# The last stage's weights made float32 a stage earlier, and operands at equal addresses

## The chip, the cores and the metric

The kernel runs on one core of a Trainium2 chip. The metric is the device time of one execution in microseconds (us); several executions are timed and their median counts.

## The reference

Eight batches of eight heads, 576 tokens of 64 values each. Keys and values are averaged over groups of 8 tokens, so each head has 72 keys. All inputs are float32 except the weights' storage: they arrive as float64 words.

```python
k_p = k.reshape(B, H, Sp, 8, D).mean(axis=3); v_p = v.reshape(B, H, Sp, 8, D).mean(axis=3)
attn = softmax(scale * q @ k_p.T)
x = (attn @ v_p)            # (4608 tokens, 512)
h = max(x @ w1, x @ w2, x @ w3)     # 512 -> 768
x = h @ w_out                       # 768 -> 512
h = x @ w_in2                       # 512 -> 2048
out = (h - tanh(h)) @ w_out2        # 2048 -> 512
```

## The kernel before

Every product is taken in three matmuls on float32r parts: an operand is split into a high part H (a cast on ScalarE) and a low part L (value minus H, on VectorE or GpSimd), and the products H·H, H·L and L·H are accumulated. A weight tile arrives as 128 x 512 float64 words (512 KB); `conv` makes it float32 with one VectorE pass for the exponent (L78), a ScalarE pass on it (L80), four VectorE passes for sign and mantissa (L81, L83, L85, L87), then the cast to H (L89) and the subtraction for L (L90, on GpSimd).

The work is in three stages, one after the other on TensorE.

- **Stage A** computes attention and the maximum of the three products, in 12 blocks of 384 tokens. `moe_group` (L476 to L482) is one group of 12 matmuls of 384 columns; a block has 18 groups. The attention's steps stand in one list, written out by hand, and `moe_part` spreads them between the groups (`pace`), about two blocks ahead; they are over before block 10 begins. A tile of 128 tokens takes four score products (`qk`, L240 and L242, added up on VectorE at L245), a softmax (L263 to L272), transposes (`tr_main` at L288, `tr_left`) and, per unit of tiles, four products with the values (`av`). The first 18 groups convert the 18 weight tiles of the three products, the last block converts the 6 tiles of `wo1`. The results h go to DRAM (`hs`).
- **Stage B** (from the heading "phase B" in the code) is the product h @ w_out in 9 blocks of 512 tokens. A block has 6 groups, one per input chunk of 128; a group is 12 matmuls of 512 columns into four PSUM banks (L592 to L594). The h tile of a group is loaded four groups ahead and split two groups ahead (`load_split`, L561, L566, L567). Between the groups `conv_c` converts the 32 weight tiles of stage C, `win` and `wout` in turn, into the 32 pairs `wt`, where they stay. The results x go to DRAM (`xs`) from four copies each block (L598 on ScalarE, L600 on VectorE).
- **Stage C** takes 9 blocks of 512 tokens, 16 chunks of 128 inner columns each. `h2` (L662 to L664) is 12 matmuls of the weights' `ct` tiles (stationary) with the x tiles `ioH` and `ioL` (moving), into one bank. `gact` makes g = h - tanh(h) on ScalarE and VectorE. `prod` (L675 to L677), three chunks later, is 12 matmuls of g (stationary) with the `ct` tiles (moving) into four banks. The x tiles of a block are split on GpSimd.

The tile framework orders the instructions of each engine from the order of the code and the readiness that its planner expects; each engine then runs its own list in order. All loads and stores are issued by one queue, SyncE's.

SBUF is filled from two sides. The left side begins behind 16,384 bytes of scratch and some constants and holds, in A, the weights of the three products, the x tiles and the conversion's tiles; in C the `ct` tiles, from byte 16,576 of each partition. The right side grows down from byte 229,344: in A all of attention, in B and C first the pool `io` (ioL, ioH, ob), then `wo` (B) or `gp` (the g tiles, C). All tiles of `io`, `wo`, `wl` and `gp` have sizes that are multiples of 512 bytes.

Of the kernel before, what the change touches and what calls it, by code (L numbers as in the profile page):

```python
# [47 lines left out]
def moe_chain_kernel(ctx, tc, qt, kt, vm, vl, ident, cst, w123, wo1, win, wout, out):  # L48
# [18 lines left out]

    # float64 words to float32, split into two float32r parts
    def conv_load(st, src):
# [3 lines left out]

    def conv(st, raw, H, L, eng):
        pe = st.tile([128, 512], I32, tag="pe", name="pe", bufs=2)
        a = st.tile([128, 512], I32, tag="ma", name="ma", bufs=2)
        lo, hi = raw[:, :, 0], raw[:, :, 1]
        V.tensor_scalar(out=pe, in0=hi, scalar1=20, scalar2=0x7FF,  # L78
                        op0=ALU.logical_shift_right, op1=ALU.bitwise_and)
        A.activation(pe, pe, AF.Relu, bias=ebias, scale=float(1 << 23))  # L80
        V.tensor_scalar(out=a, in0=hi, scalar1=3, scalar2=0x7FFFFF,  # L81
                        op0=ALU.logical_shift_left, op1=ALU.bitwise_and)
        V.scalar_tensor_tensor(out=a, in0=hi, scalar=-2147483648, in1=a,  # L83
                               op0=ALU.bitwise_and, op1=ALU.bitwise_or)
        V.scalar_tensor_tensor(out=a, in0=lo, scalar=29, in1=a,  # L85
                               op0=ALU.logical_shift_right, op1=ALU.bitwise_or)
        V.tensor_tensor(out=a, in0=a, in1=pe, op=ALU.bitwise_or)  # L87
        w = a.bitcast(F32)
        A.copy(H, w)  # L89
        eng.tensor_tensor(out=L, in0=w, in1=H.bitcast(F32), op=ALU.subtract)  # L90

# [1 line left out]
    cp = pool("cst")  # L93
    wa = pool("wa")
    xr = pool("xr", bufs=3)
    hp = pool("hp", bufs=4)
    sta = pool("sta")
    at = pool("at", side="right")

# [16 lines left out]

    # attention units: (first token, tiles of tokens); a tile is (batch, first token in batch, count)
    units = []
# [199 lines left out]

    # one list of steps for the whole attention, in the order in which they are issued
    steps = []  # L320
# [84 lines left out]
    for o in tail:  # L405
        add(*o)
    # v of a batch may be replaced once its last product is issued
    done_at = {}
# [15 lines left out]

    # startup
    for t in (kbd[0], VX, VH, VL, kbd[1]):
# [18 lines left out]
    def conv_next():  # L445
        i = nconv[0]
        if i < 18:
            conv(sta, raws.pop(i), wH[i].rearrange("p a b -> p (a b)"),
                 wL[i].rearrange("p a b -> p (a b)"), G)
            nconv[0] += 1  # L450
            if i + 2 < 18:
                raws[i + 2] = conv_load(sta, w123[i + 2])

    first_av = next(i for i, (f, _) in enumerate(steps) if f is av)
# [33 lines left out]

    def moe_part(groups, upto):
        """groups of products, with the attention's steps up to upto spread over them"""  # L490
        first = pos[0]

        def pace(x):
            attn_to(first + (upto - first) * x // (2 * len(groups)))

        for k, (j, f, m) in enumerate(groups):
            conv_next()
            moe_group(j, f, m, lambda: pace(2 * k + 1))
            pace(2 * k + 2)
# [6 lines left out]
    def point(x):  # L506
        """the step at which the attention is x blocks far"""
        j = int(x)
        if j >= NA - 1:
            return len(steps) - 1  # L510
        lo = block_end[j - 1] if j else -1
        return int(lo + (block_end[j] - lo) * (x - j)) if x > j else lo
# [4 lines left out]
    for j in range(2, NA - 1):  # L517
        moe_part(gr(j), point(j + 2 + LEAD))
    attn_to(len(steps) - 1)
    close("at")  # L520
    io = pool("io", side="right")
# [15 lines left out]
    for nme in ("sta", "hp", "xr", "wa"):  # L537
        close(nme)

# [1 line left out]
    wl = pool("wl")  # L541
    stb = pool("stb", side="right")
    wt = [(wl.tile([128, 512], F32R, name=f"ctH{c}"), wl.tile([128, 512], F32R, name=f"ctL{c}"))
          for c in range(2 * NC2)]
    # pairs in the order of use: input chunk c, output chunk c
    srcs = [(win if c % 2 == 0 else wout)[c // 2] for c in range(2 * NC2)]
    raws = {i: conv_load(stb, srcs[i]) for i in range(2)}
    nconv = [0]

    def conv_c():  # L550
        i = nconv[0]
        if i < 2 * NC2:
            conv(stb, raws.pop(i), wt[i][0], wt[i][1], G)
            nconv[0] += 1
            if i + 2 < 2 * NC2:
                raws[i + 2] = conv_load(stb, srcs[i + 2])

# [14 lines left out]
    def hsrc(j, kc):  # L572
        g, o = divmod(j * BB, HG)
        return hs[g][kc][:, o:o + BB]

    loads = [(j, kc) for j in range(NB) for kc in range(NF)]
    AHEAD, SPL = 4, 2
# [5 lines left out]
    for i, (j, kc) in enumerate(loads):  # L583
        if kc == 0:
            acc = [psm.tile([128, 512], F32, tag="mm", name="ps_mm") if j % 2 == 0 else
                   ps2.tile([128, 512], F32, tag="sc" if e < 2 else "tr", name="ps_acc") for e in range(NE)]
# [15 lines left out]
        if i + AHEAD < len(loads):  # L602
            lt[i + AHEAD] = load_split(hsrc(*loads[i + AHEAD]), V)
        while nconv[0] < min(2 * NC2, (i + 1) * 2 * NC2 // (len(loads) - 2)):
            conv_c()
    close("stb")
    close("wo")
# [3 lines left out]

# [1 line left out]
    gp = pool("gp", bufs=2, side="right")  # L613
    xl_ = [(j, kc) for j in range(NB) for kc in range(NE)]
    lt = {}
    nld, nsp = [0], [0]

    def c_load():
        i = nld[0]
        if i < len(xl_):  # L620
            j, kc = xl_[i]
            lt[i] = load_split(xs[j][kc], G)
            nld[0] += 1

    def c_split():
        i = nsp[0]
        if i < len(xl_):
            lt[i][1]()
            nsp[0] += 1

    def gact(ps):
# [25 lines left out]
    def h2(j, c):  # L657
        ps = psc.tile([128, 512], F32, tag="mm", name="ps_mm", bufs=3)
        wh, wl_ = (t.rearrange("p (a b) -> p a b", b=128) for t in wt[2 * c])
        for kc in range(NE):  # L660
            xh, xl2 = lt[j * NE + kc][0]
            T.matmul(ps, wh[:, kc], xh, start=(kc == 0), stop=False)  # L662
            T.matmul(ps, wh[:, kc], xl2, start=False, stop=False)  # L663
            T.matmul(ps, wl_[:, kc], xh, start=False, stop=(kc == NE - 1))  # L664
        return ps
# [20 lines left out]

    for _ in range(4):
        c_load()
    for _ in range(4):
        c_split()  # L690
    seq = [(j, c) for j in range(NB) for c in range(NC2)]
    for i in range(len(seq) + LAG):
# [5 lines left out]
        if i < len(seq):  # L698
            gs[j, c] = gact(ps)
            if c == 2:  # L700
                for _ in range(NE):
                    c_load()
            if 6 <= c < 10:
                c_split()
            if c == NC2 - 1:
                for k in range(NE):
                    lt.pop(j * NE + k)
    for nme in ("psc", "gp", "io", "wl", "cst"):
        close(nme)
# [54 lines left out]
```

## Time and profile before

| | |
|---|---|
| Median of 3 runs | 1609.07 us (1609.0 to 1609.45) |
| Profiled execution, first to last instruction | 1608.5 us |
| Busy: TensorE / VectorE / ScalarE / GpSimd | 1548.1 / 1215.2 / 836.4 / 223.7 us |
| Mean granted TensorE clock | 0.990 |
| Moved by DMA | 117.87 MB |

The span of the profile is the time on the core between the first and the last instruction; around it lie 0.6 us up to the median of the timed runs. Matmuls are pipelined, so that TensorE's busy time counts overlaps of neighbours; the distance from one start to the next tells more. "Granted clock" is the share of full speed (2.4 GHz) that the throttle lets through; its other level is 0.5.

### The profile page before, as it was taken

To read this page: it belongs to the slowest core of one execution; us is meant where nothing else is said; L and a number is where in the kernel's file an instruction comes from. 1 tells how busy PE (TensorE), PEld (TensorE's weight loads), DVE (VectorE), ACT (ScalarE), POOL (GpSimd) and SP (SyncE) were. 2 spreads that over 40 slices of the span, in tenths; PEclk is the share of its full clock that TensorE was granted. 3 is DMA by queue.
4 is the path that set the end of the run, shared out by engine and by line. 5 is a ranking of instruction groups with operands and counts; after the bars stand their busy time and mean duration, and the time that the engine had idled before them with its cause. 6 is when DMAs were issued, how large, how long until landed. Compare 5 with 4: busy or idle time off the path is not lost.

```text
span 1608.5 us, 21497 instructions
## 1 busy us (share of the span) xinstructions
PE 1548.1 (96%) x7540; PEld 1337.7 (83%) x7540; DVE 1215.2 (76%) x2131; ACT 836.4 (52%) x2081; POOL 223.7 (14%) x245
## 2 busy tenths in 40 slices
PE   4789999999999999998899999999999999999999
PEld 4688999999999999876688888888888888888887
DVE  8999565555555663999588878788888888887886
ACT  5565455545545521444465555555555555555554
POOL 5351210202010011332301001010101001010000
PEclk9899999999999999999999999999999999999999
DMA  7455232212121232676500001010100000010000
GB/s 236 158 161 163 84 99 79 87 45 75 42 65 39 67 120 77 230 241 234 198 1 27 26 2 52 1 53 0 33 21 27 26 27 27 1 54 0 27 1 27
DMA packets 61997, 117.87 MB, mean 73 GB/s; under 512 B 10816, under 2 KB 20160, under 8 KB 61888
## 3 DMA queue, kind: packets, MB, share of 16 engines
q1 hardware_dynamic: 61888, 116.49, 21.8%
q8 instruction: 59, 0.97, 0.3%
q14 instruction: 50, 0.41, 0.1%
HBM read 83.43 MB, written 33.03 MB: 72 GB/s over the span
## 4 chain that ended last, share of the span: by engine, by line
PE 50%; DVE 0%; issue 0%
PE ps_mm L663 8%; PE ps_mm L662 8%; PE ps_mm L664 8%; PE ps_acc L676 8%; PE ps_acc L675 8%; PE ps_acc L677 8%; DVE ob L683 0%
## 5 line engine op out<-in xcount | busy, mean ns | idle before, releaser
L476 PE MATMUL ps_mm<-xH,wH 128*128 128x384 f32 x864 | 304.5, 353 | 5.3 <-ACT wH L89 4.5
L477 PE MATMUL ps_mm<-xL,wH 128*128 128x384 f32 x864 | 292.4, 339 | 1.0 <-DVE xL L317 1.0
L478 PE MATMUL ps_mm<-xH,wL 128*128 128x384 f32 x864 | 292.7, 339 | 0.6 <-POOL wL L90 0.6
L650 ACT CAST gH<-w 128x512 fp32r<-128x512 f32 x144 | 89.4, 621 | 297.0 <-DVE w L649 297.0
L662 PE MATMUL ps_mm<-ioH,ctH 128*128 128x512 f32 x576 | 228.3, 396 | 5.3 <-ACT ob L598 5.3
L663 PE MATMUL ps_mm<-ioL,ctH 128*128 128x512 f32 x576 | 229.1, 398 | 0.0
L664 PE MATMUL ps_mm<-ioH,ctL 128*128 128x512 f32 x576 | 228.5, 397 | 0.0
L675 PE MATMUL ps_acc<-ctH,gH 128*128 128x512 f32 x576 | 228.1, 396 | 0.0
L676 PE MATMUL ps_acc<-ctL,gH 128*128 128x512 f32 x576 | 227.9, 396 | 0.0
L677 PE MATMUL ps_acc<-ctH,gL 128*128 128x512 f32 x576 | 227.9, 396 | 0.0
L651 DVE TENSOR_TENSOR gL<-w,gH 128x512 fp32r<-128x512 f32 x144 | 104.1, 723 | 92.5 <-ACT gH L650 92.3
L476 PEld LDWEIGHTS ps_mm<-xH,wH 128*128 128x128 f32 x864 | 164.7, 191 | 7.2 <-ACT wH L89 4.8
L477 PEld LDWEIGHTS ps_mm<-xL,wH 128*128 128x128 f32 x864 | 164.6, 191 | 1.9 <-DVE xL L317 1.7
L478 PEld LDWEIGHTS ps_mm<-xH,wL 128*128 128x128 f32 x864 | 163.7, 189 | 1.5 <-POOL wL L90 1.5
L567 POOL TENSOR_TENSOR ioL<-ioL,ioH 128x512 fp32r<-128x512 f32 x36 | 53.5, 1509 | 666.9 <-ACT ioH L566 666.9
L662 PEld LDWEIGHTS ps_mm<-ioH,ctH 128*128 128x128 f32 x576 | 108.6, 189 | 32.2 <-ACT ob L598 5.7
L663 PEld LDWEIGHTS ps_mm<-ioL,ctH 128*128 128x128 f32 x576 | 108.7, 189 | 27.1
L664 PEld LDWEIGHTS ps_mm<-ioH,ctL 128*128 128x128 f32 x576 | 108.8, 189 | 26.0
L675 PEld LDWEIGHTS ps_acc<-ctH,gH 128*128 128x128 f32 x576 | 108.2, 188 | 26.5
L677 PEld LDWEIGHTS ps_acc<-ctH,gL 128*128 128x128 f32 x576 | 108.2, 188 | 26.5
L676 PEld LDWEIGHTS ps_acc<-ctL,gH 128*128 128x128 f32 x576 | 108.2, 188 | 25.8
L482 DVE TENSOR_TENSOR h<-h,ps_mm 128x384 f32<-128x384 f32 x144 | 79.0, 549 | 66.0 <-PE ps_mm L478 59.2
(108 smaller groups left out, 2924.9 us busy)
## 6 DMA issues: line engine op xcount, KB each, us to landing
hs<-h SPq DMA_DIRECT2D x72, 192.0 KB, 1.9
ioL<-hs SPq DMA_DIRECT2D x54, 256.0 KB, 4.2
kraw<-kt SPq DMA_DIRECT2D x32, 288.0 KB, 3.9
raw<-w SPq DMA_DIRECT2D x18, 512.0 KB, 3.5
xs<-ob SPq DMA_DIRECT2D x36, 256.0 KB, 2.6
ioL<-xs SPq DMA_DIRECT2D x36, 256.0 KB, 3.0
out<-ob SPq DMA_DIRECT2D x36, 256.0 KB, 2.2
qraw<-qt SPq DMA_DIRECT2D x32, 256.0 KB, 2.7
```

The costliest lines, as they stand in the source:

```text
L476: T.matmul(ps[:, :BA], wH[i][:, kc], xh[:, kc], start=(kc == 0), stop=False)
L477: T.matmul(ps[:, :BA], wH[i][:, kc], xl[:, kc], start=False, stop=False)
L478: T.matmul(ps[:, :BA], wL[i][:, kc], xh[:, kc], start=False, stop=(kc == NE - 1))
L482: V.tensor_tensor(out=t, in0=t, in1=ps[:, :BA], op=ALU.max)
L650: A.copy(gH, w)
L651: V.tensor_tensor(out=gL, in0=w, in1=gH.bitcast(F32), op=ALU.subtract)
L662: T.matmul(ps, wh[:, kc], xh, start=(kc == 0), stop=False)
L663: T.matmul(ps, wh[:, kc], xl2, start=False, stop=False)
L664: T.matmul(ps, wl_[:, kc], xh, start=False, stop=(kc == NE - 1))
L675: T.matmul(acc, gH[:, r], oh, start=(c == 0), stop=False)
L676: T.matmul(acc, gH[:, r], ol, start=False, stop=False)
L677: T.matmul(acc, gL[:, r], oh, start=False, stop=(c == NC2 - 1))
```

## The change

`conv` is cut in two: `conv_bits` makes the float32 word on VectorE and ScalarE, and the split into H and L is apart. In stage A a new `conv_store` loads the raw words of stage C's weights, makes them float32 and stores them to DRAM (`wsc`, 256 KB a tile); it is called before every fourth group of blocks 2 to 10. In stage B `w_load` brings one such tile a group into the place of its L part, and `w_split` casts it (ScalarE) and subtracts (GpSimd).

The loads and splits of stage C's first x tiles move into the last groups of B, where nothing of h is left to load, and these four are subtracted on VectorE. The accumulators of B's blocks swap their two sets of PSUM banks, so that the last block uses the other four.

The scratch at the start of SBUF goes from 16,384 to 1,024 bytes, and a pad of 72 float32 words is put at the outer end of the right side.

```diff
@@ -65,13 +65,17 @@
     hs = [dr.tile([NF, 128, HG], F32, name=f"hs{i}") for i in range(NT // HG)]
     xs = [dr.tile([NE, 128, BB], F32, name=f"xs{i}") for i in range(NB)]

+    srcs = [(win if c % 2 == 0 else wout)[c // 2] for c in range(2 * NC2)]
+    wsc = [dr.tile([128, 512], F32, name=f"wsc{i}") for i in range(2 * NC2)]
     def conv_load(st, src):
         raw = st.tile([128, 512, 2], I32, tag="raw", name="raw", bufs=2)
         Q.dma_start(out=raw.bitcast(I64).rearrange("p n o -> p (n o)"), in_=src)
         return raw

-    def conv(st, raw, H, L, eng):
+    def conv_bits(st, raw):
         pe = st.tile([128, 512], I32, tag="pe", name="pe", bufs=2)
         a = st.tile([128, 512], I32, tag="ma", name="ma", bufs=2)
         lo, hi = raw[:, :, 0], raw[:, :, 1]
...
@@ -85,16 +89,21 @@
         V.scalar_tensor_tensor(out=a, in0=lo, scalar=29, in1=a,
                                op0=ALU.logical_shift_right, op1=ALU.bitwise_or)
         V.tensor_tensor(out=a, in0=a, in1=pe, op=ALU.bitwise_or)
-        w = a.bitcast(F32)
+        return a
+    def conv(st, raw, H, L, eng):
+        w = conv_bits(st, raw).bitcast(F32)
         A.copy(H, w)
         eng.tensor_tensor(out=L, in0=w, in1=H.bitcast(F32), op=ALU.subtract)

     cp = pool("cst")
     wa = pool("wa")
     xr = pool("xr", bufs=3)
     hp = pool("hp", bufs=4)
     sta = pool("sta")
+    pool("rp", side="right").tile([128, 72], F32, name="rpad")
     at = pool("at", side="right")

     consts = cp.tile([128, 12], F32, name="consts")
...
@@ -450,6 +459,19 @@
             nconv[0] += 1
             if i + 2 < 18:
                 raws[i + 2] = conv_load(sta, w123[i + 2])
+    nws = [0, 0]
+    craw = {}
+    def conv_store():
+        i = nws[0]
+        if i < 2 * NC2:
+            craw[i] = conv_load(sta, srcs[i])
+            nws[0] += 1
+        i = nws[1]
+        if i in craw and (i + 1 in craw or nws[0] == 2 * NC2):
+            Q.dma_start(out=wsc[i], in_=conv_bits(sta, craw.pop(i)).bitcast(F32))
+            nws[1] += 1

     first_av = next(i for i, (f, _) in enumerate(steps) if f is av)
     attn_to(NP)
...
@@ -495,6 +517,8 @@

         for k, (j, f, m) in enumerate(groups):
             conv_next()
+            if store and k % store == store - 1:
+                conv_store()
             moe_group(j, f, m, lambda: pace(2 * k + 1))
             pace(2 * k + 2)

...
@@ -515,8 +539,10 @@
     moe_part(gr(1, 0, HF), point(2.5))
     moe_part(gr(0, HF, NF) + gr(1, HF, NF), point(3 + LEAD))
     for j in range(2, NA - 1):
-        moe_part(gr(j), point(j + 2 + LEAD))
+        moe_part(gr(j), point(j + 2 + LEAD), 4)
     attn_to(len(steps) - 1)
+    while nws[1] < 2 * NC2:
+        conv_store()
     close("at")
     io = pool("io", side="right")
     wo = pool("wo", side="right")
...
@@ -537,23 +563,24 @@
     for nme in ("sta", "hp", "xr", "wa"):
         close(nme)

     wl = pool("wl")
-    stb = pool("stb", side="right")
     wt = [(wl.tile([128, 512], F32R, name=f"ctH{c}"), wl.tile([128, 512], F32R, name=f"ctL{c}"))
           for c in range(2 * NC2)]
-    srcs = [(win if c % 2 == 0 else wout)[c // 2] for c in range(2 * NC2)]
-    raws = {i: conv_load(stb, srcs[i]) for i in range(2)}
-    nconv = [0]
-    def conv_c():
-        i = nconv[0]
+    nw = [0, 0]
+    def w_load():
+        i = nw[0]
         if i < 2 * NC2:
-            conv(stb, raws.pop(i), wt[i][0], wt[i][1], G)
-            nconv[0] += 1
-            if i + 2 < 2 * NC2:
-                raws[i + 2] = conv_load(stb, srcs[i + 2])
+            Q.dma_start(out=wt[i][1].bitcast(F32), in_=wsc[i])
+            nw[0] += 1
+    def w_split():
+        i = nw[1]
+        h, l = wt[i]
+        A.copy(h, l.bitcast(F32))
+        G.tensor_tensor(out=l, in0=l.bitcast(F32), in1=h.bitcast(F32), op=ALU.subtract)
+        nw[1] += 1

     def load_split(src, eng):
         l = io.tile([128, 512], F32R, tag="L", name="ioL", bufs=8)
...
@@ -572,6 +599,23 @@
     def hsrc(j, kc):
         g, o = divmod(j * BB, HG)
         return hs[g][kc][:, o:o + BB]
+    xl_ = [(j, kc) for j in range(NB) for kc in range(NE)]
+    ct = {}
+    nld, nsp = [0], [0]
+    def c_load(eng):
+        i = nld[0]
+        if i < len(xl_):
+            j, kc = xl_[i]
+            ct[i] = load_split(xs[j][kc], eng)
+            nld[0] += 1
+    def c_split():
+        i = nsp[0]
+        if i < len(xl_):
+            ct[i][1]()
+            nsp[0] += 1

     loads = [(j, kc) for j in range(NB) for kc in range(NF)]
     AHEAD, SPL = 4, 2
...
@@ -582,7 +626,7 @@
         lt[i][1]()
     for i, (j, kc) in enumerate(loads):
         if kc == 0:
-            acc = [psm.tile([128, 512], F32, tag="mm", name="ps_mm") if j % 2 == 0 else
+            acc = [psm.tile([128, 512], F32, tag="mm", name="ps_mm") if j % 2 else
                    ps2.tile([128, 512], F32, tag="sc" if e < 2 else "tr", name="ps_acc") for e in range(NE)]
         (h, l), _ = lt.pop(i)
         if i + SPL < len(loads):
...
@@ -601,33 +645,21 @@
                 Q.dma_start(out=xs[j][e], in_=ob)
         if i + AHEAD < len(loads):
             lt[i + AHEAD] = load_split(hsrc(*loads[i + AHEAD]), V)
-        while nconv[0] < min(2 * NC2, (i + 1) * 2 * NC2 // (len(loads) - 2)):
-            conv_c()
-    close("stb")
+        else:
+            c_load(V)
+        if i >= len(loads) - 2:
+            c_split()
+            c_split()
+        w_load()
+        while nw[1] < min(2 * NC2, i * 2 * NC2 // (len(loads) - 4)):
+            w_split()
     close("wo")
     close("ps2")
     close("psm")
     psc = pool("psc", space=PS)

     gp = pool("gp", bufs=2, side="right")
-    xl_ = [(j, kc) for j in range(NB) for kc in range(NE)]
-    lt = {}
-    nld, nsp = [0], [0]
-    def c_load():
-        i = nld[0]
-        if i < len(xl_):
-            j, kc = xl_[i]
-            lt[i] = load_split(xs[j][kc], G)
-            nld[0] += 1
-    def c_split():
-        i = nsp[0]
-        if i < len(xl_):
-            lt[i][1]()
-            nsp[0] += 1
     def gact(ps):
         u = gp.tile([128, 512], F32, tag="u", name="u")
         th = gp.tile([128, 512], F32, tag="th", name="th")
...
@@ -658,7 +690,7 @@
         ps = psc.tile([128, 512], F32, tag="mm", name="ps_mm", bufs=3)
         wh, wl_ = (t.rearrange("p (a b) -> p a b", b=128) for t in wt[2 * c])
         for kc in range(NE):
-            xh, xl2 = lt[j * NE + kc][0]
+            xh, xl2 = ct[j * NE + kc][0]
             T.matmul(ps, wh[:, kc], xh, start=(kc == 0), stop=False)
             T.matmul(ps, wh[:, kc], xl2, start=False, stop=False)
             T.matmul(ps, wl_[:, kc], xh, start=False, stop=(kc == NE - 1))
...
@@ -684,10 +716,6 @@
                 r0 = j * BB + t * 128
                 Q.dma_start(out=out[r0:r0 + 128, :], in_=ob)

-    for _ in range(4):
-        c_load()
-    for _ in range(4):
-        c_split()
     seq = [(j, c) for j in range(NB) for c in range(NC2)]
     for i in range(len(seq) + LAG):
         if i < len(seq):
...
@@ -699,13 +727,13 @@
             gs[j, c] = gact(ps)
             if c == 2:
                 for _ in range(NE):
-                    c_load()
+                    c_load(G)
             if 6 <= c < 10:
                 c_split()
             if c == NC2 - 1:
                 for k in range(NE):
-                    lt.pop(j * NE + k)
-    for nme in ("psc", "gp", "io", "wl", "cst"):
+                    ct.pop(j * NE + k)
+    for nme in ("psc", "gp", "io", "rp", "wl", "cst"):
         close(nme)


...
@@ -753,7 +781,7 @@
         "w123": c(w123), "wo1": c(moe_w_out).view(np.int64).reshape(NF, 128, 512),
         "win": cols(moe2_w_in), "wout": c(moe2_w_out).view(np.int64).reshape(NC2, 128, 512),
     }
-    nc = bacc.Bacc("TRN2", target_bir_lowering=False, num_devices=1)
+    nc = bacc.Bacc("TRN2", target_bir_lowering=False, num_devices=1, dynamic_dma_scratch_size=1024)
     args = [nc.dram_tensor(n, a.shape, mybir.dt.from_np(a.dtype), kind="ExternalInput").ap()
             for n, a in arrays.items()]
     out = nc.dram_tensor("out", (NT, DM), F32, kind="ExternalOutput").ap()
```

The hunks left out, and the lines taken out of these, change comments and blank lines alone.

## Rows read from the trace of the kernel before

**Rows 1.** Stretches: start:end, us, busy us (instructions) per engine, granted clock, DMA share, GB/s

```profile
core 0 of [0], span 1608.5 us
core 0: us, PE busy (x) PEld busy (x) DVE busy (x) ACT busy (x) POOL busy (x), PEclk, DMA share, GB/s
98.00:132.00 34.00, 28.15 (x167) 26.81 (x167) 33.75 (x63) 18.04 (x50) 11.19 (x9) 1.00 0.46 150
136.00:171.30 35.30, 35.25 (x212) 34.82 (x211) 29.13 (x66) 20.00 (x70) 8.29 (x16) 1.00 0.55 170
171.30:547.50 376.20, 374.58 (x2292) 367.21 (x2292) 210.88 (x511) 195.60 (x786) 37.00 (x71) 1.00 0.20 62
...
628.00:789.80 161.80, 152.71 (x650) 120.28 (x648) 148.13 (x213) 72.55 (x124) 48.94 (x33) 1.00 0.65 224
801.50:1603.00 801.50, 801.50 (x3437) 644.62 (x3436) 658.03 (x1024) 440.69 (x765) 44.81 (x29) 1.00 0.06 20
```

**Rows 2.** Timeline of TensorE late in stage B: start, us, engine and line

```profile
785.69 0.39 PE L592 MATMUL ps_mm<-ioH,woH 128*128 128x512 f32 x1
...
789.54 0.39 PE L594 MATMUL ps_mm<-ioH,woL 128*128 128x512 f32 x1
```

**Rows 3.** Timeline at the last boundary, in brackets the idle time before

```profile
790.88 3.30 ACT L566 CAST ioH<-ioL 128x512 fp32r<-128x512 f32 x5 [6.17 <-DMA ioL<-xs]
794.09 1.07 ACT L598 COPY ob<-ps_mm 128x512 f32<-128x512 f32 x2
...
795.21 0.79 PE L662 MATMUL ps_mm<-ioH,ctH 128*128 128x512 f32 x1 [5.27 <-ACT ob L598]
```

**Rows 4.** Waits of the weight queue in stage B: us, times, longest

```profile
PEld ps_mm L593 <- DVE ioL L567: 7.3, 8, 1.9
PEld ps_acc L593 <- DVE ioL L567: 7.0, 8, 1.8
```

**Rows 5.** The stretch around the last boundary

```profile
760.00:800.00 40.00, 32.84 (x129) 25.25 (x128) 25.14 (x37) 17.33 (x31) 16.02 (x12) 0.93 0.62 217
```

**Rows 6.** Timeline of TensorE in the middle of stage C

```profile
1099.79 0.39 PE L662 MATMUL ps_mm<-ioH,ctH 128*128 128x512 f32 x1
...
1116.59 0.39 PE L662 MATMUL ps_mm<-ioH,ctH 128*128 128x512 f32 x1
```

**Rows 7.** Timeline of TensorE in stage A's block 11, without attention

```profile
595.86 0.33 PE L476 MATMUL ps_mm<-xH,wH 128*128 128x384 f32 x1
...
605.22 0.33 PE L476 MATMUL ps_mm<-xH,wH 128*128 128x384 f32 x1
```

**Rows 8.** Groups of the conversion: busy us, mean ns of one, idle before

```profile
L85 DVE SCALAR_TENSOR_TENSOR ma<-raw,ma 128x512 int32<-128x512 int32 x56 | 47.3, 845 | 0.7
L83 DVE SCALAR_TENSOR_TENSOR ma<-raw,ma 128x512 int32<-128x512 int32 x56 | 44.2, 789 | 1.1
L80 ACT ACTIVATE pe<-pe,consts 128x512 int32<-128x512 int32 x56 | 40.4, 727 | 49.5 <-DVE pe L78 49.4
L87 DVE TENSOR_TENSOR ma<-ma,pe 128x512 int32<-128x512 int32 x56 | 38.8, 693 | 0.6
L81 DVE TENSOR_SCALAR ma<-raw 128x512 int32<-128x512 int32 x56 | 37.5, 670 | 2.7 <-POOL woL L90 1.4 <-POOL ctL L90 1.2
L78 DVE TENSOR_SCALAR pe<-raw 128x512 int32<-128x512 int32 x56 | 26.1, 466 | 6.7 <-DMA raw<-win 4.3 <-DMA raw<-wout 2.0 <-DMA raw<-wo 0.5
```

**Rows 9.** A stretch of stage C, for its DMA share and rate

```profile
960.00:1000.00 40.00, 40.00 (x173) 32.16 (x172) 33.98 (x51) 23.40 (x42) 6.19 (x4) 1.00 0.15 53
```

**Rows 10.** TensorE's waits in 171.3:547.5, 136:171.3 and 98:132, one row each

```profile
PE ps_tr L288 <- DVE sc L270: 1.5, 3, 0.6
...
PEld ps_tr L299 <- ACT lf L272: 0.3, 1, 0.3
...
PE ps_sc L240 <- DVE sc L245: 5.6, 2, 3.5
```

**Rows 11.** Instructions of line 87 alone in two stretches of stage A

```profile
98.00:132.00 34.00, 4.43 (x7) 1.00 0.46 150
136.00:171.30 35.30, 1.36 (x2) 1.00 0.55 170
```

More of the change, by code (lines that the diff above doesn't have):

```diff
@@ L487, in moe_chain_kernel, with moe_part @@
     hsb = {}
-    def moe_part(groups, upto):
+    def moe_part(groups, upto, store=0):
         first = pos[0]
```

## The prediction

> **What bounds the kernel now.** I read the busy times by stage first [rows 1]. TensorE is the bound in stage A (blocks 2 to 9 there, 374.58 of 376.20 us) and without a gap in stage C (801.50 of 801.50 us); VectorE is not (658.03 of 801.50 us in C). Stage B differs: TensorE 152.71 and VectorE 148.13 of 161.80 us. Its matmul busy time is padded by overlap, so the second view is the step from one matmul start to the next.
>
> In the timeline of B, 17 steps take 789.54 - 785.69 = 3.85 us, 0.2265 us each [rows 2]. At that step its 54 x 12 = 648 matmuls need 146.8 us, yet from 628.0 [rows 1] to the first matmul of C at 795.21 [rows 3] it lasts 167.2 us. The waits say why: TensorE's weight queue stands for DVE's L567, the low half of the h tiles [rows 4], because five VectorE passes of each weight conversion lie in front of it. At the boundary TensorE ends at about 789.9 and starts at 795.21: ACT has stood 6.17 us for the loads of x, splits five tiles, and only then copies the accumulator whose bank C's first product needs [rows 3]. The pause drops the granted clock: 0.93 over 760 to 800 [rows 5], a loss of 0.07 x 40 = 2.8 us at the lower level.
>
> The third view is the step of C: 16.80 us from one L662 to the one three chunks (72 matmuls) later, 0.2333 us [rows 6], 6.8 ns more than B's for the same 512 columns. Stage A's is (605.22 - 595.86) / 54 = 0.1733 us for 384 columns [rows 7]. From A to B 128 columns more cost 53.2 ns, 0.416 ns a column (one column a cycle at the 2.4 GHz level); so A and B share a fixed 13.7 ns, and C has 20.5. What differs is not the pattern (B and the second product of C both take three matmuls per bank, two on one stationary operand). It is where the operands lie: in A both of a product lie on the left side of SBUF or both on the right, in B both on the right, in C one on each. By the kernel's allocation the left starts at 192 and the right at 480 modulo 512, 32 bytes apart modulo 64; tiles between keep these residues.
>
> **The change, part by part.** *B loses the conversions' five VectorE passes.* They take 0.466 + 0.670 + 0.789 + 0.845 + 0.693 = 3.46 us each [rows 8]: 32 of them are 111 of VectorE's 148 us in B [rows 1], which leaves 37 plus four x splits. ScalarE loses 32 x 0.727 = 23 of 72.55 us; the copy and GpSimd's subtraction remain. So TensorE is the only engine that can bound B. The loads don't: B moves 54 h loads, 32 weight loads, 36 stores and 4 x loads of 256 KB, 33 MB, and in stage C the queue shows 53 GB/s at a share of 0.15 [rows 9], some 350 GB/s if full: about 94 us as an estimate, behind 147. In SP's queue the weight loads stand between h loads; the h load is issued four groups of 2.7 us ahead, and the first weight load waits for A's last matmul, at a time when four h tiles are already in. Gain: 167.2 - 146.8 = 20.4 us; I give 1 us back for its first loads.
>
> *The boundary.* x of block 0 is loaded at B's groups 50 to 53 and split at 52 and 53, and the last accumulator uses the other four banks than C's first products. TensorE then goes on without a pause; that was in the 20.4, and the 2.8 us of clock come on top. If a split is late, some of the 5.3 us of the old wait come back.
>
> *Equal residues.* The scratch shrinks by 15,360 = 30 x 512 bytes, so the left stays at 192; the 288-byte pad moves the right from 480 to 192. The operands of C then stand to each other as those of A and B do. No row prices this directly. From below: nothing, if the offset is not the cause. From above: C's step becomes B's, 3456 x (0.2333 - 0.2265) = 23.6 us. I take the upper end, because A and B, of different shapes, agree on the fixed part, and no other difference of C separates it from both. A and B keep equal residues and their steps.
>
> *A gains 32 conversions.* A call stands before every fourth group of blocks 2 to 10; the first only loads, so 31 conversions fall in blocks 2 to 9, beside attention, and the last in block 10, beyond the end of the attention list, where VectorE has room. VectorE goes from 210.88 to 210.88 + 31 x 3.46 = 318 of 376.20 us, 85%; ScalarE from 52 to 58%. On the path is only what delays TensorE: a score product waits for VectorE's sum of two products before, the transposes for the softmax's last multiplication (L270), which is already late three times [rows 10]. From below: 136 to 171.3 has two conversions [rows 11] and VectorE at 29.13 of 35.30 us (83%), and TensorE's weight queue waited 0.3 us in all [rows 10]. From above: 98 to 132 has seven, VectorE at 33.75 of 34.00, and TensorE waited 5.6 us [rows 10], 0.8 us a conversion, 25 us for 31. The new stage is at the load of the first, so I take 0.2 us each, 6 us. In SP's queue each store of a converted tile waits for L87, and the q, k and v loads and the h stores behind it wait too; a q load has a whole tile of some 13 us before its split, and h has four buffers, so this hides unless VectorE falls a tile behind. The extra 25 MB are 67 GB/s beside 62 [rows 1].
>
> **Sum.** 1608.5 - 20.4 + 1 - 2.8 - 23.6 + 6 = 1568.7 us by the profiled execution; the median of the runs is 1609.07, 0.6 more, so 1569 us.
>
> **Rivals.** *The step of C does not move.* For it: the fixed part could come from what is special to C, operands written by ScalarE and VectorE just before, 658 us of VectorE work beside, or the distance of some 100 KB between operands. Against: B has those writers and a busier VectorE. Time: 1569 + 23.6 = 1592 us. The Trainium skill's page "TensorE: Matmul & The Clock Gate" (Part 2, step 1) would have this: TensorE has two independent SBUF read ports, and loading the next weights takes no bandwidth from the running matmul. By that rule a relation between the two addresses can't matter; the rows, with two fixed parts for one shape, show that something does, without naming it.
>
> *A pays as in its first conversions*: 0.8 us each, 25 instead of 6 us, 1588 us. For it: chains of attention tolerate little. Against: the load of 83% without such waits.
>
> *The other side: VectorE becomes the bound of A.* The planner's order puts whole conversions in front of softmax steps, and at 85% VectorE never catches up within a tile. Full price 31 x 3.46 = 107 us, 1670 us. It decides from (1609 - 1569 + 6) / 31 = 1.5 us a conversion. Against: even at 99% load it was 0.8.
>
> **How the numbers follow.** Forecast 0.62 (1563 to 1577 alone), the step of C unmoved 0.20, A at the high price 0.12, VectorE the bound of A or two of these together 0.06. The range runs from 1561 (A free, B whole) to 1596 (C unmoved and a little more in A). A change within 0.2% (3 us) can't be told from none here. Faster 0.92, same 0.03, slower 0.05.
>
> **What would show it.** C's L662 to the third next in 16.3 us where it took 16.80, and B's step unchanged; B from its first matmul to C's in about 147 us, without a wait for L567 and with a granted clock of 1.00 across; blocks 2 to 9 within some 10 us of 376, VectorE near 318. Wrong: a C step of 0.233, or waits of the transposes (L288) and score products (L240) on VectorE that add up to tens of us.

## The result, and the profile after

The changed kernel takes 1594.29 us (median of 3 runs, 1593.19 to 1594.65) where the kernel before takes 1609.07: a ratio of 0.9906 [0.9891, 0.9921], 14.8 us faster. The sign is the one forecast and the time lies in the range; the gain is 15 us where 40 were forecast. Its profiled span is 1591.4 us, 17.1 less than before.

The starts of the stages, read from the timelines of both kernels, say where it went (us):

| | before | changed | length before | length changed |
|---|---|---|---|---|
| stage A, block 2 | 171.5 | 170.8 | 47.5 | 54.4 |
| block 3 | 219.0 | 225.1 | 46.8 | 62.4 |
| block 4 | 265.8 | 287.5 | 45.9 | 47.2 |
| block 5 | 311.7 | 334.7 | 47.5 | 53.4 |
| blocks 6 to 11 | 359.2 | 388.0 | 268.9 | 267.3 |
| stage B | 628.1 | 655.3 | 167.1 | 147.9 |
| stage C | 795.2 | 803.2 | 809.0 | 783.2 |
| last matmul | 1604.2 | 1586.4 | | |

B gives 19.2 us and C 25.8 us; A takes 27.2 back, all of it in blocks 2 to 5, although the conversions are called from block 2 to block 10. Of C's 25.8 us some 3 are the granted clock just behind the old pause, which in the kernel before read:

```profile
795.00:800.00 5.00, 4.79 (x11) 3.80 (x12) 0.00 (x0) 0.67 (x2) 4.00 (x4) 0.50 0.79 262
800.00:805.00 5.00, 5.00 (x20) 3.95 (x19) 3.35 (x7) 3.42 (x7) 0.00 (x0) 0.87 0.01 2
```

Stretches of the changed kernel, columns as in [rows 1]:

```profile
core 0 of [0], span 1591.4 us
core 0: us, PE busy (x) PEld busy (x) DVE busy (x) ACT busy (x) POOL busy (x), PEclk, DMA share, GB/s
171.00:345.00 174.00, 153.55 (x882) 148.03 (x881) 160.44 (x350) 92.22 (x325) 26.57 (x40) 0.95 0.65 208
345.00:550.00 205.00, 204.04 (x1246) 199.56 (x1246) 112.08 (x273) 105.58 (x424) 16.35 (x32) 1.00 0.17 54
655.00:803.00 148.00, 147.37 (x651) 121.73 (x649) 56.21 (x70) 61.91 (x104) 48.37 (x34) 1.00 0.65 212
803.00:1586.00 783.00, 782.80 (x3454) 648.21 (x3455) 653.37 (x1026) 439.23 (x767) 46.68 (x30) 1.00 0.06 22
```

The part of stage A that gets the conversions has come apart into two halves. From 171 to 345 us VectorE is busy 160.44 of 174 us (92%), TensorE only 153.55, at a granted clock of 0.95 and with 208 GB/s on the queues. From 345 to 550 VectorE is at 55%, about its share in the kernel before [rows 1], and TensorE runs through. Stage B is TensorE's alone now: VectorE is down from 148.13 us [rows 1] to 56.21. In C the shares of VectorE and ScalarE are within 2% of what they were, and the stage is shorter.

The last pass of a conversion (L91) alone, with its counts, in three stretches of the changed kernel:

```profile
core 0: us, DVE busy (x), PEclk, DMA share, GB/s
150.00:345.00 195.00, 24.41 (x34) 0.96 0.66 208
345.00:585.00 240.00, 0.00 (x0) 1.00 0.16 50
585.00:655.00 70.00, 2.72 (x4) 1.00 0.22 74
```

Of the 34 in the first stretch 32 are stage C's weights (two are the last of the three products' weights), and the 4 in the third are weights of B. So all 32 ran by 339 us, one in some 5.9 us, and none where more than half of the calls stand.

Waits in 171 to 345 us of the changed kernel, TensorE's and then VectorE's (us in total, times, longest):

```profile
PE ps_sc L249 <- DVE sc L254: 5.8, 3, 3.1
PE ps_tr L297 <- DVE sc L279: 5.5, 2, 4.0
PE ps_tr L297 <- ACT pe L84: 4.2, 1, 4.2
PE ps_tr L308 <- DVE xL L326: 3.3, 3, 2.0
PE ps_tr L297 <- DVE xL L326: 1.6, 1, 1.6
...
DVE pe L82 <- DMA raw<-wout: 5.1, 4, 2.2
DVE pe L82 <- DMA raw<-win: 2.8, 3, 1.4
```

TensorE's five rows add up to 20.4 us, where before the same stretch had 0.6. Four of them name VectorE. The third names ScalarE's pass of a conversion, which a transpose does not read; what stands just ahead on VectorE tells more. VectorE's timeline of the changed kernel, idle time in brackets:

```profile
252.12 0.18 DVE L278 RECIPROCAL su<-su 64x8 f32<-64x8 f32 x1
254.51 0.43 DVE L82 TENSOR_SCALAR pe<-raw 128x512 int32<-128x512 int32 x1 [2.22 <-DMA raw<-wout]
254.86 0.74 DVE L279 TENSOR_TENSOR sc<-sc,su 64x576 f32<-64x576 f32 x1
```

And TensorE's, in the same place:

```profile
255.75 0.66 PE L297 MATMUL ps_tr<-idt,sc 64*128 64x64 f32 x4 [4.22 <-ACT pe L84]
```

The softmax has its reciprocal at 252.3, and its last multiplication (L279) could follow. In VectorE's list a conversion's first pass (L82) stands between them, and that one waits 2.22 us for its raw words. The multiplication ends at 255.60, and the transposes (L297) start at 255.75, after 4.22 us: 0.15 us behind its end, as in the waits of 1.5 and 4.0 us whose rows name L279 itself. A wait for memory of an instruction that nobody needs soon has become a wait of TensorE.

Not every wait of TensorE has VectorE standing still in front of it. Ahead of the one of 4.0 us VectorE works without a gap, and passes of conversions (L85 to L91) hold up the softmax (L278, L279); the last line is TensorE's:

```profile
335.06 1.20 DVE L87 SCALAR_TENSOR_TENSOR ma<-raw,ma 128x512 int32<-128x512 int32 x1
...
336.65 0.79 DVE L89 SCALAR_TENSOR_TENSOR ma<-raw,ma 128x512 int32<-128x512 int32 x1
...
337.77 1.05 DVE L91 TENSOR_TENSOR ma<-ma,pe 128x512 int32<-128x512 int32 x1
338.74 0.95 DVE L279 TENSOR_TENSOR sc<-sc,su 128x576 f32<-128x576 f32 x1
339.83 0.63 PE L297 MATMUL ps_tr<-idt,sc 128*128 128x128 f32 x4 [3.96 <-DVE sc L279]
```

Three waits of TensorE, 8.9 of the 20.4 us (those that end at 180.38, 237.57 and 255.75), have VectorE standing for raw words during them or up to 1.3 us before them; it stood 2.45, 1.42 and 2.22 us. In front of the other 11.5 us VectorE stood for no transfer longer than 0.2 us within the last 4 us.

The step of C, by the timeline of TensorE from one first product to the one three chunks on, as in [rows 6]:

```profile
1099.78 0.39 PE L694 MATMUL ps_mm<-ioH,ctH 128*128 128x512 f32 x1
...
1116.10 0.39 PE L694 MATMUL ps_mm<-ioH,ctH 128*128 128x512 f32 x1
```

16.32 us for 72 matmuls, 0.2267 us each, where [rows 6] has 0.2333.

The boundary from B to C, TensorE and ScalarE, to be held against [rows 3]:

```profile
801.77 0.58 ACT L642 COPY ob<-ps_acc 128x512 f32<-128x512 f32 x1 [0.76 <-PE ps_acc L638]
801.98 0.39 PE L638 MATMUL ps_acc<-ioH,woL 128*128 128x512 f32 x1
802.41 0.62 ACT L593 CAST ioH<-ioL 128x512 fp32r<-128x512 f32 x1
803.20 0.47 PE L694 MATMUL ps_mm<-ioH,ctH 128*128 128x512 f32 x1 [0.83 <-ACT ioH L593]
```

The pause is 0.83 us instead of 5.27. The row names a cast of x (L593), which stands in ScalarE's list behind a copy of B's accumulator that has waited 0.76 us for its last product. That cast is of a tile of C's second block (its subtraction is one of three on GpSimd; the four tiles of the first block are split by 795.6 us), which the first product doesn't read. VectorE's copy of the last accumulator ends at 803.10, so it may be what is left of the wait; that is not shown.

### The profile page after: what moved, and what is told of

Read it like the earlier page. It is cut to its first block, busy times and chain, and to the rows that moved or that the text cites. A ratio compares the mean times of both kernels' runs of the same rounds, so it can differ in the third digit from the quotient of the medians.

```text
span 1591.4 us, 21589 instructions
## 1 busy us (share of the span) xinstructions
PE 1527.2 (96%) x7540; PEld 1345.8 (85%) x7540; DVE 1192.1 (75%) x2135; ACT 834.0 (52%) x2081; POOL 222.8 (14%) x241
## 4 chain that ended last, share of the span: by engine, by line
PE 79%; DVE 15%; DMA 3%; issue 1%; ACT 1%; POOL 1%; SPq 0%; DVEq 0%; ACTq 0%; POOLq 0%
PE ps_mm L694 8%; PE ps_acc L709 8%; PE ps_mm L696 8%; PE ps_acc L707 8%; PE ps_mm L695 8%; PE ps_acc L708 8%; PE ps_mm L498 6%; PE ps_mm L500 6%; PE ps_mm L499 6%; DVE ma L89 2%; DVE ma L87 2%; PE ps_acc L638 2%; PE ps_acc L636 2%; PE ps_acc L637 2%; DVE h L504 1%; DVE ma L91 1%
## 5 line engine op out<-in xcount | busy, mean ns | idle before, releaser
L498 PE MATMUL ps_mm<-xH,wH 128*128 128x384 f32 x864 | 307.9, 357 | 3.3 <-ACT wH L96 3.3
L499 PE MATMUL ps_mm<-xL,wH 128*128 128x384 f32 x864 | 295.7, 342 | 0.2 <-DVE xL L326 0.2
L694 PE MATMUL ps_mm<-ioH,ctH 128*128 128x512 f32 x576 | 224.2, 389 | 0.8 <-ACT ioH L593 0.8
L695 PE MATMUL ps_mm<-ioL,ctH 128*128 128x512 f32 x576 | 224.1, 389 | 0.0
L696 PE MATMUL ps_mm<-ioH,ctL 128*128 128x512 f32 x576 | 224.1, 389 | 0.0
L707 PE MATMUL ps_acc<-ctH,gH 128*128 128x512 f32 x576 | 224.1, 389 | 0.0
L708 PE MATMUL ps_acc<-ctL,gH 128*128 128x512 f32 x576 | 224.1, 389 | 0.0
L709 PE MATMUL ps_acc<-ctH,gL 128*128 128x512 f32 x576 | 224.1, 389 | 0.0
L498 PEld LDWEIGHTS ps_mm<-xH,wH 128*128 128x128 f32 x864 | 167.1, 193 | 4.7 <-ACT wH L96 3.7
L594 POOL TENSOR_TENSOR ioL<-ioL,ioH 128x512 fp32r<-128x512 f32 x32 | 49.2, 1556 | 728.7 <-ACT ioH L593 728.7
```

The source lines that it names most:

```text
L498: T.matmul(ps[:, :BA], wH[i][:, kc], xh[:, kc], start=(kc == 0), stop=False)
L499: T.matmul(ps[:, :BA], wH[i][:, kc], xl[:, kc], start=False, stop=False)
L707: T.matmul(acc, gH[:, r], oh, start=(c == 0), stop=False)
L708: T.matmul(acc, gH[:, r], ol, start=False, stop=False)
L709: T.matmul(acc, gL[:, r], oh, start=False, stop=(c == NC2 - 1))
```

## The experiments

Each ratio is against the kernel before, run beside the experiment. "A ends" is the start of the first matmul of B: 628.1 us in the kernel before, 655.3 in the changed kernel.

**Which part gives what.** The residues alone, in the kernel before:

```diff
+    pool("rp", side="right").tile([128, 72], F32, name="rpad")
...
-    nc = bacc.Bacc("TRN2", target_bir_lowering=False, num_devices=1)
+    nc = bacc.Bacc("TRN2", target_bir_lowering=False, num_devices=1, dynamic_dma_scratch_size=1024)
```

> The kernel before with the smaller scratch and the pad alone. If the residues of the operands set stage C's step: the step falls from 0.2333 to 0.2267 us, 3456 steps give 23 us, so about 1586 us, with stages A and B as before. If C's step came from its writers or from the boundary's pause (the rival of the prediction): 0.2333 us and 1609 us.

Measured 1585.57 us, 0.986 [0.9845, 0.9874]. The group of C's first product, on the page of this run (us busy, mean ns of one, idle time before):

```profile
L663 PE MATMUL ps_mm<-ioH,ctH 128*128 128x512 f32 x576 | 225.5, 392 | 4.9 <-ACT ob L599 4.9
```

The old wait at the boundary is still there (4.9 us), and stage B is as long as before; in the middle of C 96 matmuls take 21.76 us (1098.21 to 1119.97), 0.2267 each. The two edits that move addresses and nothing else give 23 us. The rest of the change, all that moves work, costs some 8 us on top of them (0.9906 against 0.986).

**Are the conversions' passes the loss in A?** The changed kernel without the passes; loads and stores stay:

```diff
-            Q.dma_start(out=wsc[i], in_=conv_bits(sta, craw.pop(i)).bitcast(F32))
+            craw.pop(i)
+            Q.dma_start(out=wsc[i], in_=fix)
```

> The changed kernel without the five VectorE passes and the ScalarE pass of stage A's 32 conversions: the raw loads and the stores stay, and a constant is stored, so that the output is not the reference's. If VectorE's load is what holds stage A back: A ends at about 628 us instead of 655, the total is about 1567 us. If it is the loads and stores (25 MB more, and SyncE's queue): A stays at about 650 us or more, total about 1590 us.

Measured 1578.79 us, 0.9819 [0.9804, 0.9833]. A ends at 642.4, neither at 628 nor at 655. The 14 us all fall in block 2, which lasts 64.0 us instead of 47.5; blocks 3 to 11 run as before. With nothing to hold the raw buffers their loads came in a burst, and VectorE's timeline there shows who stood for it:

```profile
219.85 0.43 DVE L82 TENSOR_SCALAR pe<-raw 128x512 int32<-128x512 int32 x1 [14.96 <-DMA raw<-wo]
```

This is a conversion of B's weights (`wo1`), called in block 11 and put into VectorE's list in block 2; behind it TensorE waits 11.7 us for a score sum. As a test of the transfers against the passes the run decides nothing, since leaving the passes out changed the transfers too. It shows the mechanism of 252 us again, larger. A ends 12.9 us earlier than in the changed kernel; what part of its loss the passes are can't be told from that.

**Spread out.** The changed kernel, with one pass of a conversion a group, each pinned in VectorE's list behind the group's maximum; the loads, passes and stores are the same, one call in every group instead of every fourth:

```diff
+    def conv_store():
+        with tc.issue_after(last_max[0].ins):
+            next(ps_it, None)
...
-            V.tensor_tensor(out=t, in0=t, in1=ps[:, :BA], op=ALU.max)
+            last_max[0] = V.tensor_tensor(out=t, in0=t, in1=ps[:, :BA], op=ALU.max)
...
-        moe_part(gr(j), point(j + 2 + LEAD), 4)
+        moe_part(gr(j), point(j + 2 + LEAD), 1)
```

(`ps_it` yields after each of the five passes; ScalarE's pass goes with the first, the store with the last.)

> The changed kernel, but each of the five passes of a conversion is put in VectorE's order behind the maximum of another group, one pass a group over blocks 2 to 10. If the harm is that the conversions are bunched into 153 to 338 us: A ends at 628 to 636 us, total 1567 to 1575 us. If a conversion costs its 0.85 us wherever it stands: A at 655 us, total about 1594 us.

Measured 1564.64 us, 0.9733 [0.9718, 0.9747], 1.9% below the changed kernel; no kernel here is faster beyond the intervals. Its stretch 171 to 549:

```profile
171.00:549.00 378.00, 374.84 (x2291) 366.86 (x2290) 279.70 (x652) 212.57 (x815) 39.74 (x70) 1.00 0.38 119
```

Its waits of TensorE in the same stretch:

```profile
PE ps_tr L297 <- DVE sc L279: 2.6, 5, 0.7
PE ps_av L318 <- DVE xL L326: 0.3, 1, 0.3
PE ps_sc L249 <- DVE sc L254: 0.3, 1, 0.3
```

A ends at 628.9, 0.8 us later than before, for the same 32 conversions and the same 25 MB; they run some 13 us apart, from 172 to 586. So the passes as such and their transfers cost A next to nothing: where they stand in the list does. VectorE is busy 279.70 us where it was 210.88 [rows 1], with some 28 conversions in the stretch: 2.4 us of busy time each.

**Does the place of the calls count?**

```diff
-        moe_part(gr(j), point(j + 2 + LEAD), 4)
+        moe_part(gr(j), point(j + 2 + LEAD), 8)
```

> The changed kernel with the calls at every eighth group instead of every fourth. If the planner runs a conversion as soon as its raw words are there, whatever the place of the call: the conversions stay between 153 and 340 us, A ends at 655 us, total 1594 us within 2 us. If the place of the call decides: the first sixteen spread out to 547 us, the rest follows behind, A's stretch to 345 us loses half of its 27 us, total about 1580 us.

Measured 1597.2 us, 0.9931 [0.9914, 0.9948]. Now 18 calls stand in blocks 2 to 10, and the last 15 conversions are called behind block 10. They ran where they ran before:

```profile
150.00:345.00 195.00, 24.35 (x34) 0.96 0.65 207
345.00:585.00 240.00, 0.00 (x0) 1.00 0.16 50
```

A ends at 659.2, 3.9 us later than with a call at every fourth group, for a reason that is not shown; the total is 1 us outside the first expectation. The order of VectorE's list is not that of the code: what the planner expects to be ready is put in early, however late it is called.

**The run of five passes, or the distance?** The kernel of one pass a group, but five together behind every fifth maximum:

```diff
-        with tc.issue_after(last_max[0].ins):
-            next(ps_it, None)
+        if ngrp[0] % 5 == 0:
+            with tc.issue_after(last_max[0].ins):
+                for _ in range(5):
+                    next(ps_it, None)
+        ngrp[0] += 1
```

> As the kernel with one pass a group, but the five passes of a conversion stand together behind one maximum, at every fifth group: the same mean spacing (13 us a conversion), in runs of 3.46 us. If VectorE's load in a stretch is what counts: A ends at 628 to 632 us, total 1564 to 1568 us. If a run of five passes in front of the softmax is what costs: 0.3 us or more a conversion, A at 637 us or later, total 1573 us or more.

Measured 1567.07 us, 0.9741 [0.9727, 0.9756]; A ends at 629.7. Five passes in one piece (3.0 us by their means in this run) are borne at this distance. The same total of passes twice as dense, two in every group:

```diff
         with tc.issue_after(last_max[0].ins):
             next(ps_it, None)
+            next(ps_it, None)
```

> As the kernel with one pass a group, but two passes a group: the conversions are over by block 6, 6 us apart as in the changed kernel, yet pinned behind maxima, so that none should stand for its raw words. If VectorE's load in the stretch is the cause: 56% of the stretch plus 3.46 of every 6.5 us is over 100%, A loses 15 to 28 us again, total 1580 to 1592 us. If the changed kernel lost its time because VectorE stood in order for raw words that had not landed: A loses under 5 us, total under 1570 us.

Measured 1577.18 us, 0.9804 [0.9789, 0.9818]; A ends at 639.7, 11.6 us late, between the two expectations. The stretch 171 to 345 of the two runs, five together first:

```profile
171.00:345.00 174.00, 171.91 (x1042) 167.94 (x1041) 132.44 (x298) 94.23 (x356) 22.40 (x38) 1.00 0.42 131
```

and two a group:

```profile
171.00:345.00 174.00, 167.99 (x1015) 162.90 (x1014) 156.54 (x352) 99.86 (x366) 24.93 (x39) 1.00 0.58 185
```

At 76% VectorE costs TensorE nothing that counts; at 90%, with conversions 6.6 us apart and still held in their places, A ends 11.6 us late. The second run is not free of standing for raw words, as it was meant to be; two rows of VectorE's waits in its stretch:

```profile
DVE pe L476 <- DMA raw<-wout: 3.5, 2, 3.1
DVE pe L476 <- DMA raw<-win: 0.7, 1, 0.7
```

**The raw words.** The changed kernel with four raw buffers:

```diff
-        raw = st.tile([128, 512, 2], I32, tag="raw", name="raw", bufs=2)
+        raw = st.tile([128, 512, 2], I32, tag="raw", name="raw", bufs=4)
```

> The changed kernel with four buffers for the raw words instead of two: loads go further ahead, while the conversions keep nearly the places that they have in VectorE's order (18 to 59 maxima in). If the stretch is lost to VectorE's load: A ends at 650 to 658 us and the total stays at 1588 to 1597 us. If it is lost because VectorE stands in its order for raw words (8 us of its time, with the stops and clock drops behind them): A ends at 635 to 645 us, total 1575 to 1585 us.

Measured 1585.69 us, 0.9848 [0.9832, 0.9865]; A ends at 651.0, 4.3 us earlier than in the changed kernel. VectorE's waits for raw words are gone from 171 to 345, the load is not (first line). But VectorE now stands as long for something else, the store of an earlier converted tile whose buffer the next one needs (second line, of its waits in the same stretch):

```profile
171.00:345.00 174.00, 154.81 (x903) 148.54 (x903) 159.48 (x356) 94.89 (x341) 28.38 (x40) 0.97 0.66 207
DVE ma L85 <- DMA wsc<-ma: 8.0, 5, 4.7
```

In the changed kernel the raw words took 7.9 us of VectorE's time there and the stores 0.7. So the run exchanges one wait for another, and doesn't separate standing from load; the end of A lies in the first range expected, the total in neither.

**How equal must the residues be?** The kernel of one pass a group with another pad; only the right side moves:

```diff
-    pool("rp", side="right").tile([128, 72], F32, name="rpad")
+    pool("rp", side="right").tile([128, 80], F32, name="rpad")
```

and 88, 104 and 136 words, so that the two sides stand 32, 64, 128 and 256 bytes apart modulo 512.

> The kernel with one pass a group, with a pad of 80 words instead of 72: the right side stands 32 bytes off the left modulo 64, as it did in the kernel before. If the residue modulo 64 sets the step of stage C: 0.2333 us again, 23 us more, total about 1588 us. If the smaller scratch or something else brought the faster step: 0.2267 us, 1565 us.

> The same with a pad of 88 words: the two sides are 64 bytes apart modulo 512, but equal modulo 64. If equality modulo 64 is enough: a step of 0.2267 us, total about 1565 us. If the addresses must be equal modulo more (128 to 512 bytes): a slower step, up to 0.2333 us and 1588 us.

> The kernel with one pass a group, with a pad of 104 words: the two sides are 128 bytes apart modulo 512. If equality modulo 128 is enough: a step of 0.2267 us in stage C and about 1565 us. If the residues must agree modulo 256 or 512: about 0.2325 us, as with 64 bytes, and about 1586 us.

> The same with a pad of 136 words: the two sides are 256 bytes apart modulo 512. If equality modulo 256 is enough, as the products of attention suggest (their two operands are 256 bytes apart modulo 512, and they step by 0.174 us for 384 columns): 0.2267 us and about 1565 us. If it must be modulo 512: about 0.2325 us and 1586 us.

Step: from C's first matmul to its last, by their count.

| apart modulo 512 | us | ratio | step of C, us |
|---|---|---|---|
| 0 (72 words) | 1564.64 | 0.9733 [0.9718, 0.9747] | 0.2267 |
| 32 | 1590.87 | 0.9887 [0.9872, 0.9902] | 0.2334 |
| 64 | 1586.94 | 0.9864 [0.9848, 0.9881] | 0.2325 |
| 128 | 1587.76 | 0.9867 [0.9851, 0.9884] | 0.2331 |
| 256 | 1564.88 | 0.9727 [0.9712, 0.9741] | 0.2267 |

The group of C's first product at 32 bytes:

```profile
L719 PE MATMUL ps_mm<-ioH,ctH 128*128 128x512 f32 x576 | 228.2, 396 | 0.8 <-ACT ioH L618 0.8
```

and at 256 bytes:

```profile
L719 PE MATMUL ps_mm<-ioH,ctH 128*128 128x512 f32 x576 | 224.2, 389 | 0.8 <-ACT ioH L618 0.8
```

Stages A and B, whose operands lie on one side, end within 2 us of each other in all five. B's operands both lie on the side that moves, and its matmul is the same in each; at 32 bytes:

```profile
L662 PE MATMUL ps_acc<-ioL,woH 128*128 128x512 f32 x120 | 46.7, 389 | 0.0
```

So what counts is where the two operands stand to each other, and not the address of that side by itself. 32 bytes apart give back the step of the kernel before. Equality modulo 64 or 128 is not enough; modulo 256 it is.

**The boundary.** The kernel of one pass a group, with the loads and splits of C's first x tiles behind B again, on GpSimd, and the old bank sets:

```diff
-        else:
-            c_load(V)
-        if i >= len(loads) - 2:
-            c_split()
-            c_split()
...
+    for _ in range(4):
+        c_load(G)
+    for _ in range(4):
+        c_split()
     seq = [(j, c) for j in range(NB) for c in range(NC2)]
```

> The kernel with one pass a group, with the x loads and splits of stage C's first block behind stage B again, on GpSimd, and the PSUM banks of B's blocks as before. If the boundary's part is worth what the prediction gave it: TensorE stands some 5 us at the boundary and the clock falls, 5 to 9 us more, 1570 to 1574 us. If the wait went away with the conversions alone: 1565 us.

Measured 1566.46 us, 0.9732 [0.9717, 0.9746], the same as with the moved loads. The first matmul of C:

```profile
776.27 0.47 PE L714 MATMUL ps_mm<-ioH,ctH 128*128 128x512 f32 x1 [0.83 <-ACT ioH L618]
```

The pause is 0.83 us here too, without a drop of the clock. Moving the loads, and the other banks, are worth nothing that can be measured. What remains to have removed the 5.3 us of before is that the conversions left B (with them in B, in the run of the addresses alone, 4.9 us stayed): without them the planner brings these loads and splits forward by itself, to the same pause.

## Why the prediction was right, and where it failed

*B without the passes*: right. From B's first matmul to C's it lasts 147.9 us where 147 were given, TensorE has no wait in it, and the low half of h (L567 before) is no longer waited for. The transfers hide behind it as said: share 0.65, 212 GB/s.

*The boundary*: right in the sum, not in the reason. 4.4 of 5.3 us are gone, and the drop of the clock with them (1.00 from 655 on). But the step credited the moved loads and the swapped banks, and the last experiment takes both back at no cost.

*Equal residues*: right, at the upper end that was taken. C's step is 0.2267, B's 0.2265; 3456 x (0.2333 - 0.2267) = 22.8 us, and the residues alone gave 23. The rival in which the step does not move is out. The rule of the Trainium skill's page "TensorE: Matmul & The Clock Gate" (Part 2, step 1), by which the two operands come through independent ports, does not describe this: moving one side by 32, 64 or 128 bytes and nothing else makes the same matmul 5.8 to 6.7 ns longer.

*A gains 32 conversions*: this step failed, 6 us forecast, 27.2 measured. It took the calls' spacing, one every fourth group to block 9, for the spacing on VectorE, and so a load of 85% over 376 us. The conversions stood in VectorE's list as early as the planner thought them ready, and all ran by 339 us. There VectorE's own work of 55% [rows 1] meets at least 2.4 us of busy time (the price with one pass a group) in every 5.9, 41%: about all that the engine has. Measured, it is busy 92% of the stretch and stands another 5% for raw words and stores. (The 3.46 us of the prediction are the sum of mean durations, most of them from stage B. In the changed kernel's stretch the five means add up to 3.0 us, and neighbouring passes overlap.) Blocks 2 to 5 lose 29.5 us. As an estimate, TensorE's waits in 171 to 345 are 20.4 of them, and the lower level of the clock after its stops another 0.05 x 174 = 8.7.

A full VectorE alone does not say what a block loses. Block 4 loses 1.3 us with VectorE busy 46.13 of 47.20 us:

```profile
287.50:334.70 47.20, 46.01 (x279) 45.44 (x278) 46.13 (x101) 27.81 (x99) 6.65 (x11) 1.00 0.66 211
```

Block 3, which loses 15.6 us, has it busy 56.17 of 62.40 us. What decides beside the load, the order of passes and softmax steps or the times that VectorE stands still, was not tried apart.

Put in the place of the 6, the 27.2 give 1568.7 + 21.2 = 1590 us by the profiled span, against 1591.4. The other terms stand by their size, the boundary's for another reason than the one given. That the time lies in the range is luck: the upper end of 1596 was set for a C whose step stays. At the spacing that the step assumed, its price was even high: one pass a group costs A 0.8 us in all.

The rival *A pays as in its first conversions* named the size (0.8 us each, 25 us; measured 0.85). It was given 0.12, because the load was reckoned at 85%. The row that it came from, 98 to 132 with VectorE at 99% [rows 1], was the right one for a bunch. That the sizes agree so well is in part luck: the 0.8 are waits alone, while here the waits are 0.64 each and the clock brings the rest. *VectorE becomes the bound of A* came true in part, in blocks 2 to 5 and not for good, since the passes run out; its 3.46 us each were never paid in full.

How the 27 us divide is settled only in part. Passes that are pinned, at 6.6 us a conversion and with 4.2 us of standing for raw words left, cost 11.6 us. In the changed kernel 8.9 of the 20.4 us of TensorE's waits come with VectorE standing for raw words. Four raw buffers give back 4.3 us by the ends of A in the profiled executions, 8.6 us by the medians, but put standing for stores in the place of standing for raw words. What load, order, standing still and clock are worth each stays open.

## What to carry to other kernels

Work that is moved into the gaps of an engine lands where the planner puts it, not where it is called: reckon the load of the stretch in which it can become ready, and pin each piece to an instruction of the stage if the spacing matters (27 us without, 0.8 us with it). An off-path instruction that waits for a load holds up all that stands behind it on its engine; when a wait names an engine whose output the waiting instruction doesn't read, look at what stood in front of the real producer. And before moving work at all, compare the matmul step of the stages at equal shape: here two edits of addresses were worth 23 us, as much as all the moved work at its best (21 us, from 1585.57 to 1564.64).

## What the runs showed of the hardware

Which SBUF addresses the two operands of a matmul have to each other changes its step: 0.2267 us for 512 columns where the start addresses agree modulo 256 (0 and 256 bytes apart), 0.2325 to 0.2334 us at 32, 64 and 128 bytes. That holds for float32r operands with a new weight tile for each matmul, whichever operand lies on which side. It is 2.5 to 3%, at a granted clock of 1.00, on every matmul of the stage, and no row of the profile names it as a wait: the busy time of one only goes from 389 to 396 ns. The addresses come from the kernel's allocation, since the trace doesn't show them. Why it is so, and whether other distances modulo 256 differ among themselves, stays open.
